# Tile shapes, key features and PSUM tensors of a sketched attention with an exact-GELU MLP

## Chip, cores and metric

The kernel runs on one core of a Trainium2 chip. The metric is the device time of one execution in microseconds (us); the median of three runs is given. One further execution is recorded by the hardware profiler, and all rows of engines come from that one. The engines are TensorE (PE, with its weight loads as PEld), VectorE (DVE), ScalarE (ACT), GpSimd (POOL) and SyncE (SP, which here only issues DMAs).

## The reference

```
phi(x): a = x S1^T, b = x S2^T (8 columns each); phi = all 64 products a_i b_j
kv  = sum over tokens of phi(k) v^T        (64 x 32, per batch and head)
z   = sum over tokens of phi(k)
x   = (phi(q) kv) / (phi(q) z + 1e-6)      (batch 4, heads 4, tokens 1088, head_dim 32)
h   = x' w_in                              (x' : 4352 tokens x 128, heads side by side)
out = gelu_exact(h) w_out                  (w_in 128 x 2048, w_out 2048 x 128)
```

Everything is float32; the two MLP weights and S1, S2 arrive as float64 words.

## The kernel before

**Chunks.** The 1024 main tokens of a batch are two chunks of 512, so chunks 0 to 7 are the main tokens and chunk 8 the 64 remaining tokens of all four batches (256 columns). For every chunk x^T (128 channels by tokens) is made by the attention, and then the MLP goes over 16 slices `fi` of 128 hidden features: `hidden` (L551) multiplies a slice of `w_in` with x^T into a PSUM bank and applies GELU on ACT (L558). Chunks 0 and 1 use `project` (L667) for the second product, summed in one PSUM bank over the 16 slices. Chunks 2 to 7 use seven-product blocks instead of eight (`two_products`, L624), with sums of the GELU blocks made on POOL (`token_sums`, L593 to L596) and of `w_out` (`channel_sums`), and `drain` and `combine` at the end. Chunk 8 has its own branch of `project` (L664).

**Steps.** The main loop goes over steps t, one per (chunk, fi). Chunks 0 and 1 take turns in groups of four slices (steps 0 to 31); then 16 steps per chunk. Products for the second matrix come `LAG` = 2 steps or more behind. All other work is hung on steps by hand with `at(t, ...)`: `query_turn` and `query_expand` (phi of the queries, L444, L453, L460, L474), `attend` (numerators and denominators L494, denominators copied L500, reciprocal L502, x^T L506), and for batches 1 to 3 the keys: `key_turn_blocks` (L333), `features`, that is `key_features` (products with S1 and S2 L348, the outer product L361 and L362), `add_tokens` (L383, L386), `finish_keys` (`kv_sum` L391, `kv_sum_rem` L420, `take_kv`), `turn_kv` (L429, L430). For chunk n from 3 on, t = 16 (n - 1) is the step at which chunk n - 1 begins; the odd n carry the keys of batch (n + 1) / 2, so chunk 3 those of batch 2 and chunk 5 those of batch 3.

At the end of the text each instruction is tied to the one before it on its engine, so that every engine keeps the order of the text. The framework adds the semaphores.

**Head.** Batch 0's keys and chunk 0 are written out ahead of the loop. `attend_by_token` (L520, L525, L526, L528) makes chunks 0 and 1 by token, and `turn_x` transposes them (L304) and copies the two halves of x^T with ACT (L533) and DVE (L534). `Rounding` turns float64 words of the weights into float32: fields (L252, L254, DVE), low words (L248, ACT), exponents (L260, ACT), mantissas (L268, DVE, or L265 on ACT and L266 on POOL), signs (L273, DVE), product (L278, DVE or POOL). `keep_busy` (L696) is idle work for PE.

**PSUM.** Of the eight banks `hps` holds two for `hidden`, `ops` two for sums, and `wps` two pairs (`work_banks()`; `halves` gives the two banks of a pair, `work_bank()` the first bank of a pair).

**Tile shapes.** A 128x128 matmul may be written as two over 64 columns of the weights each (`by_halves`), which the profile shows as 128*64. Each float32 matmul shows as two passes.

**Stores.** Results are turned on DVE and stored by SP (L687, L690); the last chunk is copied by DVE and ACT (L673) and stored by SP and ACT, two DMAs each (L675).

Of the kernel before, what the change touches and what calls it, by code (L numbers as in the profile page):

```python
# [8 lines left out]
FP = mybir.dt.float32  # L9
# [7 lines left out]
def kernel(  # L17
# [29 lines left out]
    JC = 4  # L47
# [31 lines left out]
    def out_bank():  # L79
        return ops.tile([128, CW], FP, name="o_ps")  # L80
# [154 lines left out]
    class Rounding:  # L235


        def __init__(self, dst):
            self.dst, self.wide = dst, dst.name in raw
            if self.wide:  # L240
                rows, n = dst.shape
                self.lo, self.hi = raw[dst.name][:, :, 0], raw[dst.name][:, :, 1]
                self.a, self.e, self.r = (mlp.tile([128, LC], U32, name=f"bits_{x}")[:rows, :n] for x in "aer")
                self.low, self.m = (mlp.tile([128, LC], FP, name=f"bits_{x}")[:rows, :n] for x in ("low", "m"))
# [55 lines left out]
    def transposed(ps, name, srcs, copy):  # L300

        n = len(srcs) * 128
        for i, s in enumerate(srcs):
            pe.transpose(ps[:, i * 128:(i + 1) * 128], in_=s, identity=ident)  # L304
        t = att.tile([128, CW], FP, name=name, bufs=3 if name == "xT" else 2)
        copy(out=t[:, :n], in_=ps[:, :n])
        return t
# [33 lines left out]

    def key_features(b, r, banks, by_pool=()):

        for i in range(2 * NCH):
            for c in range(2):
                for t in range(2):
                    at = i * 128 + c * 64
                    pe.matmul(banks[t][c * 64:(c + 1) * 64, i * 32:(i + 1) * 32],  # L348
                              lhsT=kT[r][t * 64:(t + 1) * 64, at:at + 64],
                              rhs=S12[t * 64:(t + 1) * 64, 2 * t:2 * t + 2].rearrange("p h r -> p (h r)"),  # L350
                              start=True, stop=True)

        k_p[b, r] = att.tile([128, 2, J, R, R], FP, name="k_p")
        a = att.tile([128, 2, J, 2 * R], FP, name="a_t")
        for t in (1, 0):
            ab = banks[t][:, :128].rearrange("p (n r) -> p n r", r=2 * R)
            if t in by_pool:
                act.copy(out=a[:, t], in_=ab)
                pool.tensor_mul(**spread(k_p[b, r][:, t], a[:, t, :, 0:R], a[:, t, :, R:2 * R]))
            else:  # L360
                act.copy(out=a[:, t, :, 0:R], in_=ab[:, :, 0:R])  # L361
                dve.tensor_mul(**spread(k_p[b, r][:, t], a[:, t, :, 0:R], ab[:, :, R:2 * R]))  # L362
# [65 lines left out]
    def turn_kv(b, ps, copy):  # L428
        pe.transpose(ps[:, :128], in_=kv_T[b], identity=ident)  # L429
        copy(out=kz[b].rearrange("p c n -> p (c n)"), in_=ps[:, :128])  # L430
# [55 lines left out]
    def attend(n, meanwhile=lambda: None):  # L486

        W = width[n]
        owners = [(0, W, n // NCH)] if n < NMAIN else [(i * REM, (i + 1) * REM, i % 2 * 2 + i // 2) for i in range(B)]
        banks = halves(work_banks())  # L490
        for (c0, c1, b) in owners:
            for c in range(NP):
                for r in range(2):
                    pe.matmul(banks[r][c * F:(c + 1) * F, c0:c1], lhsT=kz[b][r * F:(r + 1) * F, c, :],  # L494
                              rhs=qp[n][r * F:(r + 1) * F, c, c0:c1], start=True, stop=True)
        den = att.tile([128, CW], FP, name="den")
        for h in range(H):
            c, r = h // 2, h % 2
            at = c * F + (1 - r) * D
            act.activation(out=den[h * D:(h + 1) * D, :W], in_=banks[r][at:at + D, :W], func=ACT.Copy, bias=1e-6)  # L500
        meanwhile()
        dve.reciprocal(out=den[:, :W], in_=den[:, :W])  # L502
        xT[n] = att.tile([128, CW], FP, name="xT", bufs=3)
        for h in range(H):
            rows = slice(h * D, (h + 1) * D)
            dve.tensor_mul(out=xT[n][rows, :W], in0=banks[h % 2][rows, :W], in1=den[rows, :W])  # L506
# [23 lines left out]

    def turn_x(n, ps):
        def by_both(out, in_):
            by_act(out=out[:, :CW // 2], in_=in_[:, :CW // 2])  # L533
            by_dve(out=out[:, CW // 2:], in_=in_[:, CW // 2:])  # L534

        xT[n] = transposed(ps, "xT", [x_tok[n][:, j].rearrange("p h d -> p (h d)") for j in range(JC)], by_both)

# [47 lines left out]
    def token_sums(n, b):  # L585

        g = blocks[n, b].rearrange("p (e two) (half x) -> p e two half x", two=2, half=2)
        a11, a21, a12, a22 = (g[:, :, k, h] for k in range(2) for h in range(2))
        s = {}
        for j, (name, dtype) in enumerate((("bits_a", U32), ("bits_e", U32), ("bits_low", FP), ("bits_m", FP))):  # L590
            t = mlp.tile([128, LC], dtype, name=name)
            s[j + 1] = (t if dtype == FP else t.bitcast(FP)).rearrange("p (e x) -> p e x", e=2)
        pool.tensor_sub(out=s[3], in0=a11, in1=a21)  # L593
        pool.tensor_add(out=s[1], in0=a21, in1=a22)  # L594
        pool.tensor_sub(out=s[2], in0=s[1], in1=a11)  # L595
        pool.tensor_sub(out=s[4], in0=a12, in1=s[2])  # L596
        sums[n, b] = s
# [57 lines left out]

    def project(n, fi):
        first, final = fi == 0, fi == NF - 1
        if first:
            o_of[n] = out_bank() if n < NMAIN else work_bank()
        g = g_of.pop((n, fi))  # L660
        if n == NMAIN:

            for i in range(B // 2):
                pe.matmul(o_of[n][:, i * 128:(i + 1) * 128], lhsT=g[:, i * 128:(i + 1) * 128], rhs=w_tile(w_out_sb, fi),  # L664
                          start=(first and i == 0), stop=final, skip_group_check=True)
            return
        pe.matmul(o_of[n], lhsT=w_tile(w_out_sb, fi), rhs=g, start=first, stop=final)  # L667

    def store(n):
        oT = mlp.tile([128, JC, d_model], FP, name="oT")  # L670
        if n == NMAIN:
            for i, (copy, eng) in enumerate(((by_dve, sp), (by_act, act))):
                copy(out=oT[:, i, :], in_=o_of[n][:, i * 128:(i + 1) * 128])  # L673
                for b in (i, i + 2):
                    eng.dma_start(out=out[b * S + MAIN:(b + 1) * S, :], in_=oT[b // 2 * REM:(b // 2 + 1) * REM, i, :])  # L675
            return
# [69 lines left out]
    banks = [hidden_bank(), hidden_bank()]  # L746
    keep_busy(1, banks[0], 128)
    attend_by_token(0, banks)
    expand_products(1)
    bank = out_bank()  # L750
    keep_busy(1, bank)
    w_out = [Rounding(w) for w in w_out_sb[:2]]
    w_out[0].low_words()
# [4 lines left out]
    w_in[1].product(pool)  # L758
    w_out[0].fields()
    turn_x(0, hidden_bank())  # L760
    keep_busy(1, bank)
    w_out[0].exponents()
    expand_copy(1, 2)
    expand_multiply(1, 0)
    w_out[0].finish()
    w_out[1].low_words()

# [9 lines left out]
    def features(b, r):  # L777
        key_features(b, r, halves(work_banks()))

    held = {}  # L780
# [18 lines left out]

    at(0, expand_copy, 1, 3)  # L800
    at(0, expand_multiply, 1, 1)
    at(1, lambda: (w_out[1].fields(), w_out[1].exponents()))
    for i, (t0, t1) in enumerate(((4, 6), (8, 10), (12, 20))):
# [18 lines left out]
    for n in range(3, NCHUNK):  # L822
# [5 lines left out]
        at(t + 2 if n > 3 else t - 2, query_expand, n)  # L828
        at(t + 5, attend, n, lambda b=b, keys=keys: [key_turn_blocks(b, r) for r in range(2) if keys])
        if keys:  # L830
            at(t + 8, widen_v_rem, b)
            for r in range(2):
                at(t + 11, features, b, r)
            for r in range(2):
                at(t + 11, add_tokens, b, r, dve)
            at(t + 16, finish_keys, b)
            at(t + 17, lambda b=b: turn_kv(b, held["kv"], by_act))
# [5 lines left out]
    for t, (n, fi) in enumerate(steps):  # L843
        if n < FAST:
            products[t + LAG].append((project, n, fi))
            if fi == NF - 1:
# [16 lines left out]
    for t in range(len(steps) + LAG):  # L863
        if t == 3:

            attend_by_token(1, halves(work_banks()), lambda: (w_out[1].mantissas(), w_out[1].signs(),
                                                              w_out[1].product(pool)))
        if t == 4:
            turn_x(1, work_bank())
            for f, *a in products[t]:  # L870
                f(*a)
        for n in drains[t]:
            drain(n)
        if t < len(steps):
            n, fi = steps[t]
            hidden(n, fi, by_halves=n >= FAST and (n < NMAIN or fi < 5))
        if t < len(steps) and FAST <= steps[t][0] < NMAIN and steps[t][1] % NB == NB - 1:
# [49 lines left out]
```

## Time and profile before

| | |
|---|---|
| median of 3 runs | 278.13 us (277.85 to 278.22) |
| profiled execution | 278.03 us |
| its span, first to last instruction | 276.2 us |
| PE busy | 269.6 us, 2209 matmuls |
| DVE, ACT, POOL busy | 151.1, 142.9, 144.8 us |
| HBM read and written | 10.90 and 2.23 MB |
| granted TensorE clock, mean | 0.998 |

The costliest groups are L551 at 128*64 (384 passes of 512 columns, 98.7 us busy), L558 (96 GELUs of 597 ns), L624 and the POOL sums of about 1.28 us each. A matmul's busy time overlaps with its neighbours'; what it costs in a full stream is read from the chain of work that ended last, where each piece is the time from the end of the one before. "Idle before" in a row is how long the engine stood ahead of that instruction, and the arrow names what it waited for.

### The profile page before, as it was taken

To read this page: it belongs to the slowest core of one execution; us is meant where nothing else is said; L and a number is where in the kernel's file an instruction comes from. 1 tells how busy PE (TensorE), PEld (TensorE's weight loads), DVE (VectorE), ACT (ScalarE), POOL (GpSimd) and SP (SyncE) were. 2 spreads that over 40 slices of the span, in tenths; PEclk is the share of its full clock that TensorE was granted. 3 is DMA by queue.
4 is the path that set the end of the run, shared out by engine and by line. 5 is a ranking of instruction groups with operands and counts; after the bars stand their busy time and mean duration, and the time that the engine had idled before them with its cause. 6 is when DMAs were issued, how large, how long until landed. Compare 5 with 4: busy or idle time off the path is not lost.

```text
span 276.2 us, 5543 instructions
## 1 busy us (share of the span) xinstructions
PE 269.6 (98%) x2209; PEld 134.9 (49%) x2209; DVE 151.1 (55%) x248; ACT 142.9 (52%) x282; POOL 144.8 (52%) x158
## 2 busy tenths in 40 slices
PE   8989999999999999999999999999999999999993
PEld 6744444543432455445444555444444454455793
DVE  6987688424953565079308965479037902750230
ACT  4683764356454634484348433674358344733441
POOL 3331000952003896457875877368766886777300
PEclk9999999999999999999999999999999999999999
DMA  6659263636201200000200001000200020011020
GB/s 210 188 155 325 47 167 62 160 76 161 42 0 29 34 16 2 2 0 1 40 0 1 2 2 34 7 0 2 38 0 2 0 40 0 1 24 18 4 38 19
DMA packets 37914, 13.49 MB, mean 49 GB/s; under 512 B 28288, under 2 KB 37248, under 8 KB 37888
## 3 DMA queue, kind: packets, MB, share of 16 engines
q1 hardware_dynamic: 37648, 13.05, 18.8%
q8 instruction: 17, 0.28, 0.5%
q10 hardware_dynamic: 240, 0.08, 0.1%
q14 instruction: 9, 0.07, 0.1%
HBM read 10.90 MB, written 2.23 MB: 48 GB/s over the span
## 4 chain that ended last, share of the span: by engine, by line
PE 96%; DVE 2%; ACT 0%; issue 0%
PE h_ps L551 43%; PE o_ps L624 27%; PE o_ps L667 10%; PE w_ps L453 3%; PE w_ps L664 3%; PE w_ps L494 2%; PE w_ps L391 1%; PE w_ps L696 1%; PE w_ps L348 1%; PE o_ps L400 1%; PE h_ps L304 1%; PE h_ps L520 0%; PE w_ps L420 0%; PE w_ps L520 0%; PE o_ps L304 0%
## 5 line engine op out<-in xcount | busy, mean ns | idle before, releaser
L551 PE MATMUL h_ps<-xT,w_in 128*64 128x512 f32 (+3 forms) x490 | 141.0, 577 | 1.1 <-DVE xT L534 1.0
L558 ACT ACTIVATE block<-h_ps 128x512 f32<-128x512 f32 (+1 forms) x112 | 63.4, 566 | 84.6 <-PE h_ps L551 83.7
L551 PEld LDWEIGHTS h_ps<-xT,w_in 128*64 128x64 f32 (+1 forms) x490 | 43.2, 146 | 38.0 <-issue 14.4
L593 POOL TENSOR_TENSOR bits_low<-block 128x512 f32<-128x512 f32 x24 | 30.8, 1284 | 52.8 <-ACT block L558 52.6
L624 PE MATMUL o_ps<-block,w_out 128*64 128x256 f32 x192 | 49.5, 380 | 0.0
L474 DVE TENSOR_TENSOR q_pT<-A_sb,w_ps 64x512 f32<-64x512 f32 x32 | 22.1, 691 | 43.0 <-ACT A_sb L460 42.3
L624 PEld LDWEIGHTS o_ps<-block,w_out 128*64 128x64 f32 x192 | 25.7, 137 | 32.4 <-issue 24.5
L594 POOL TENSOR_TENSOR bits_a<-block 128x512 f32<-128x512 f32 x24 | 30.6, 1274 | 12.9 <-ACT block L558 12.8
L667 PE MATMUL o_ps<-g,w_out 128*128 128x512 f32 x64 | 33.5, 604 | 0.0
L596 POOL TENSOR_TENSOR bits_m<-block,bits_e 128x512 f32<-128x512 f32 x24 | 30.6, 1276 | 1.9
L595 POOL TENSOR_TENSOR bits_e<-bits_a,block 128x512 f32<-128x512 f32 x24 | 30.6, 1274 | 1.9
L558 ACT ACTIVATE g<-h_ps 128x512 f32<-128x512 f32 x32 | 19.1, 596 | 21.2 <-PE h_ps L551 21.1
L502 DVE RECIPROCAL den<-den 128x512 f32<-128x512 f32 (+1 forms) x7 | 21.8, 3115 | 10.7 <-ACT den L500 10.7
L624 PE MATMUL o_ps<-bits_a,small 128*64 128x256 f32 x96 | 24.9, 382 | 0.0
L624 PE MATMUL o_ps<-bits_low,small 128*64 128x256 f32 x96 | 24.7, 380 | 0.0
L624 PE MATMUL o_ps<-block,small 128*64 128x256 f32 x96 | 24.7, 380 | 0.0
L624 PE MATMUL o_ps<-bits_m,w_out 128*64 128x256 f32 x96 | 24.6, 379 | 0.0
L624 PEld LDWEIGHTS o_ps<-block,small 128*64 128x64 f32 x96 | 13.0, 137 | 15.8 <-issue 11.7
L460 ACT COPY A_sb<-w_ps 64x512 f32<-64x512 f32 (+1 forms) x36 | 17.7, 557 | 3.1 <-PE w_ps L453 2.9
L506 DVE TENSOR_TENSOR xT<-w_ps,den 32x512 f32<-32x512 f32 (+1 forms) x28 | 18.2, 649 | 1.0
L667 PEld LDWEIGHTS o_ps<-g,w_out 128*128 128x128 f32 x64 | 11.3, 190 | 14.5 <-issue 13.6
L500 ACT ACTIVATE den<-w_ps 32x512 f32<-32x512 f32 (+1 forms) x28 | 15.6, 557 | 2.0 <-PE w_ps L494 1.7
(158 smaller groups left out, 295.9 us busy)
## 6 DMA issues: line engine op xcount, KB each, us to landing
block<-in_moe_w_in_dram SPq DMA_DIRECT2D x3, 512.0 KB, 7.9
block<-in_moe_w_out_dram SPq DMA_DIRECT2D x3, 512.0 KB, 10.6
k<-in_k_dram SPq DMA_DIRECT2D x48, 32.0 KB, 1.8
v<-in_v_dram SPq DMA_DIRECT2D x3, 512.0 KB, 4.3
q<-in_q_dram SPq DMA_DIRECT2D x24, 64.0 KB, 3.8
out_dram<-oT SPq DMA_DIRECT2D x24, 64.0 KB, 2.2
k<-in_k_dram SPq DMA_DIRECT2D x2, 256.0 KB, 3.1
q<-in_q_dram SPq DMA_DIRECT2D x2, 256.0 KB, 4.2
```

The costliest lines, as they stand in the source:

```text
L460: act.copy(out=A[g // 2][F:, g % 2, :width[n]], in_=B_of[n][g // 2][:F, g % 2, :width[n]])
L474: dve.tensor_mul(out=cols[r * F:(r + 1) * F], in0=a[:, :, r::2], in1=b[:, :, r::2])
L502: dve.reciprocal(out=den[:, :W], in_=den[:, :W])
L506: dve.tensor_mul(out=xT[n][rows, :W], in0=banks[h % 2][rows, :W], in1=den[rows, :W])
L551: pe.matmul(ps[rows, :W], lhsT=w[:, rows], rhs=xT[n][:, :W], start=True, stop=True)
L558: act.activation(out=g_of[n, fi][:, :W], in_=ps[:, :W], func=ACT.Gelu)
L593: pool.tensor_sub(out=s[3], in0=a11, in1=a21)
L594: pool.tensor_add(out=s[1], in0=a21, in1=a22)
L595: pool.tensor_sub(out=s[2], in0=s[1], in1=a11)
L596: pool.tensor_sub(out=s[4], in0=a12, in1=s[2])
L624: pe.matmul(acc[n][bank][half * 64:(half + 1) * 64, col:col + HW], lhsT=fixed, rhs=moving, start=b == 0 and e == 0 and name in "4715", sto ...
L667: pe.matmul(o_of[n], lhsT=w_tile(w_out_sb, fi), rhs=g, start=first, stop=final)
```

## The change

- `Rounding` and `token_sums` get three buffers for `bits_a` and `bits_e`; transposed tiles have the width that they need.
- `key_features` is split into `key_products` (PE) and `key_outer` (ACT and DVE), with a column offset. For batches 2 and 3 the products of both r go into one pair of banks and stand in `attend`, right after its numerators (`features_of_all` as its `meanwhile`, now ahead of the denominators); `outer_of_all` follows in the same step, t + 5, where the features were at t + 11. `key_turn_blocks` moves from inside `attend` to t - 2.
- `turn_kv` of batches 2 and 3 is two 128x64 products with the identity instead of a transpose.
- `turn_x` transposes into two PSUM tensors, one for each copying engine.
- From step 8 on `hidden` and `project` of chunks 0 and 1 are in 128x64 halves, and those of chunk 8 to its end.
- Chunk 8's results lie in two PSUM tensors; each is copied and stored with one DMA.
- The head: fields of `w_out[0]` ahead of `attend_by_token(0)`, all of chunk 1's expansion ahead of the loop, the first four `hidden` of chunk 0 ahead of `attend_by_token(1)`, the rounding of `w_out[0]` and `w_out[1]` spread around them, and the first two `project` after it.

```diff
+            self.a, self.e, self.r = (... bufs=2 if x == "r" else 3 ...)
-    def key_features(b, r, banks, by_pool=()):
+    def key_features(b, r, banks, by_pool=(), col=0):
+        key_products(r, banks, col)
+        key_outer(b, r, banks, by_pool, col)
+    def key_outer(b, r, banks, by_pool=(), col=0):
         k_p[b, r] = att.tile([128, 2, J, R, R], FP, name="k_p")
         a = att.tile([128, 2, J, 2 * R], FP, name="a_t")
         for t in (1, 0):
-            ab = banks[t][:, :128].rearrange("p (n r) -> p n r", r=2 * R)
+            ab = banks[t][:, col:col + 128].rearrange("p (n r) -> p n r", r=2 * R)
...
     def turn_kv(b, ps, copy):
+        if b < 2:
+            pe.transpose(ps[:, :128], in_=kv_T[b], identity=ident)
+        else:
+            for rows in (slice(0, 64), slice(64, 128)):
+                pe.matmul(ps[rows, :128], lhsT=kv_T[b][:, rows], rhs=ident, start=True, stop=True)
...
     def attend(n, meanwhile=lambda: None):
...
                     pe.matmul(banks[r][c * F:(c + 1) * F, c0:c1], ...)
+        meanwhile()
         den = att.tile([128, CW], FP, name="den")
         for h in range(H):
...
-        meanwhile()
         dve.reciprocal(out=den[:, :W], in_=den[:, :W])
...
+    def turn_x(n, banks):
+        xT[n] = att.tile([128, CW], FP, name="xT", bufs=3)
+        for i, ps in enumerate(banks):
+            for j in range(2):
+                pe.transpose(ps[:, j * 128:(j + 1) * 128], in_=x_tok[n][:, 2 * i + j]..., identity=ident)
+        for i, (ps, copy) in enumerate(zip(banks, (by_act, by_dve))):
+            copy(out=xT[n][:, i * 256:(i + 1) * 256], in_=ps[:, :256])
...
-    def project(n, fi):
+    def project(n, fi, by_halves=False):
-            o_of[n] = out_bank() if n < NMAIN else work_bank()
+            o_of[n] = out_bank() if n < NMAIN else [work_bank() for i in range(B // 2)]
...
+        for rows in (slice(0, 64), slice(64, 128)) if by_halves else (slice(0, 128),):
+            pe.matmul(o_of[n][rows], lhsT=w[:, rows], rhs=g, start=first, stop=final)
...
-                for b in (i, i + 2):
-                    eng.dma_start(out=out[b * S + MAIN:(b + 1) * S, :], ...)
+                eng.dma_start(out=out.rearrange("(two i s) d -> i two s d", two=2, i=2)[i, :, MAIN:S, :],
+                              in_=oT[:, i, :])
...
+    def features_of_all(b):
+        banks = halves(work_banks())
+        for r in range(2):
+            key_products(r, banks, r * 128)
+        held["keys"] = banks
+    def outer_of_all(b):
+        for r in range(2):
+            key_outer(b, r, held["keys"], (), r * 128)
+        for r in range(2):
+            add_tokens(b, r, dve)
...
-        at(t + 5, attend, n, lambda b=b, keys=keys: [key_turn_blocks(b, r) for r in range(2) if keys])
+        if keys:
+            for r in range(2):
+                at(t - 2, key_turn_blocks, b, r)
+        at(t + 5, attend, n, lambda b=b, keys=keys: keys and features_of_all(b))
         if keys:
+            at(t + 5, outer_of_all, b)
             at(t + 8, widen_v_rem, b)
-            for r in range(2):
-                at(t + 11, features, b, r)
-            for r in range(2):
-                at(t + 11, add_tokens, b, r, dve)
...
-            products[t + LAG].append((project, n, fi))
+            products[t + LAG].append((project, n, fi, t + LAG >= 8))
...
+        if t < 4:
+            hidden(0, t)
+            if t == 0:
+                w_out[0].exponents()
+                w_out[0].finish()
+                w_out[1].fields()
+            if t == 3:
+                attend_by_token(1, halves(work_banks()), lambda: (w_out[1].exponents(), w_out[1].low_words(),
+                                                                  w_out[1].mantissas(by_pool=True)))
+                w_out[1].signs()
+                w_out[1].product()
+                for u in range(4):
+                    for f, *a in products[u]:
+                        f(*a)
+            continue
         if t == 4:
-            turn_x(1, work_bank())
+            turn_x(1, [work_bank(), work_bank()])
...
-            hidden(n, fi, by_halves=n >= FAST and (n < NMAIN or fi < 5))
+            hidden(n, fi, by_halves=t >= 8)
```

More of the change, by code (lines that the diff above doesn't have):

```diff
@@ L242, in __init__ @@
                 self.lo, self.hi = raw[dst.name][:, :, 0], raw[dst.name][:, :, 1]
-                self.a, self.e, self.r = (mlp.tile([128, LC], U32, name=f"bits_{x}")[:rows, :n] for x in "aer")
+                self.a, self.e, self.r = (mlp.tile([128, LC], U32, name=f"bits_{x}", bufs=2 if x == "r" else 3)[:rows, :n]
+                                          for x in "aer")
                 self.low, self.m = (mlp.tile([128, LC], FP, name=f"bits_{x}")[:rows, :n] for x in ("low", "m"))
@@ L304, in transposed @@
             pe.transpose(ps[:, i * 128:(i + 1) * 128], in_=s, identity=ident)
-        t = att.tile([128, CW], FP, name=name, bufs=3 if name == "xT" else 2)
-        copy(out=t[:, :n], in_=ps[:, :n])
+        t = att.tile([128, n], FP, name=name, bufs=1 if name == "kT_rem" else 2)
+        copy(out=t, in_=ps[:, :n])
         return t
@@ L340, in spread, with key_products @@
                     in1=b[:, :, None, :].broadcast_to([128, n, R, R]))
-    def key_features(b, r, banks, by_pool=()):
+    def key_features(b, r, banks, by_pool=(), col=0):
+        key_products(r, banks, col)
+        key_outer(b, r, banks, by_pool, col)
+    def key_products(r, banks, col=0):
         for i in range(2 * NCH):
@@ L347, in key_features @@
                     at = i * 128 + c * 64
-                    pe.matmul(banks[t][c * 64:(c + 1) * 64, i * 32:(i + 1) * 32],
+                    pe.matmul(banks[t][c * 64:(c + 1) * 64, col + i * 32:col + (i + 1) * 32],
                               lhsT=kT[r][t * 64:(t + 1) * 64, at:at + 64],
@@ L428, in turn_kv @@
     def turn_kv(b, ps, copy):
-        pe.transpose(ps[:, :128], in_=kv_T[b], identity=ident)
+        if b < 2:
[3 more added lines that the diff above has]
+                pe.matmul(ps[rows, :128], lhsT=kv_T[b][:, rows], rhs=ident, start=True, stop=True)
         copy(out=kz[b].rearrange("p c n -> p (c n)"), in_=ps[:, :128])
@@ L529, in attend_by_token @@
                            in1=den[:, r, :, None].broadcast_to([128, JC * NP, D]))
[L531 to L536, printed above, removed]
+    def turn_x(n, banks):
+        xT[n] = att.tile([128, CW], FP, name="xT", bufs=3)
+        for i, ps in enumerate(banks):
+            for j in range(2):
+                pe.transpose(ps[:, j * 128:(j + 1) * 128], in_=x_tok[n][:, 2 * i + j].rearrange("p h d -> p (h d)"),
+                             identity=ident)
+        for i, (ps, copy) in enumerate(zip(banks, (by_act, by_dve))):
+            copy(out=xT[n][:, i * 256:(i + 1) * 256], in_=ps[:, :256])
     g_of, o_of = {}, {}
@@ L590, in token_sums @@
         for j, (name, dtype) in enumerate((("bits_a", U32), ("bits_e", U32), ("bits_low", FP), ("bits_m", FP))):
-            t = mlp.tile([128, LC], dtype, name=name)
+            t = mlp.tile([128, LC], dtype, name=name, bufs=3 if dtype == U32 else 2)
             s[j + 1] = (t if dtype == FP else t.bitcast(FP)).rearrange("p (e x) -> p e x", e=2)
@@ L663, in project @@
             for i in range(B // 2):
-                pe.matmul(o_of[n][:, i * 128:(i + 1) * 128], lhsT=g[:, i * 128:(i + 1) * 128], rhs=w_tile(w_out_sb, fi),
-                          start=(first and i == 0), stop=final, skip_group_check=True)
+                for h in range(2):
+                    at = i * 128 + h * 64
+                    pe.matmul(o_of[n][i][h * 64:(h + 1) * 64, :128], lhsT=g[:, at:at + 64], rhs=w_tile(w_out_sb, fi),
+                              start=first, stop=final)
             return
-        pe.matmul(o_of[n], lhsT=w_tile(w_out_sb, fi), rhs=g, start=first, stop=final)
+        w = w_tile(w_out_sb, fi)
+        for rows in (slice(0, 64), slice(64, 128)) if by_halves else (slice(0, 128),):
+            pe.matmul(o_of[n][rows], lhsT=w[:, rows], rhs=g, start=first, stop=final)
     def store(n):
@@ L672, in store @@
             for i, (copy, eng) in enumerate(((by_dve, sp), (by_act, act))):
-                copy(out=oT[:, i, :], in_=o_of[n][:, i * 128:(i + 1) * 128])
-                for b in (i, i + 2):
-                    eng.dma_start(out=out[b * S + MAIN:(b + 1) * S, :], in_=oT[b // 2 * REM:(b // 2 + 1) * REM, i, :])
+                copy(out=oT[:, i, :], in_=o_of[n][i][:, :128])
+                eng.dma_start(out=out.rearrange("(two i s) d -> i two s d", two=2, i=2)[i, :, MAIN:S, :],
+                              in_=oT[:, i, :])
             return
@@ L747 @@
     keep_busy(1, banks[0], 128)
+    w_out = [Rounding(w) for w in w_out_sb[:2]]
+    w_out[0].fields()
     attend_by_token(0, banks)
@@ L751 @@
     keep_busy(1, bank)
-    w_out = [Rounding(w) for w in w_out_sb[:2]]
     w_out[0].low_words()
@@ L758 @@
     w_in[1].product(pool)
-    w_out[0].fields()
-    turn_x(0, hidden_bank())
+    turn_x(0, [hidden_bank(), hidden_bank()])
     keep_busy(1, bank)
[L762 to L766, printed above, removed]
+    for i in range(2):
+        for g in range(2):
+            if i:
+                expand_copy(1, 2 + g)
+        expand_multiply(1, i)
     steps = [(n, fi) for f in range(0, NF, 4) for n in range(2) for fi in range(f, f + 4)]
@@ L798, in round_at @@
         at(t + 1, lambda: (r[0].exponents(), r[0].finish()))
-    at(0, expand_copy, 1, 3)
-    at(0, expand_multiply, 1, 1)
-    at(1, lambda: (w_out[1].fields(), w_out[1].exponents()))
     for i, (t0, t1) in enumerate(((4, 6), (8, 10), (12, 20))):
@@ L863 @@
     for t in range(len(steps) + LAG):
-        if t == 3:
-            attend_by_token(1, halves(work_banks()), lambda: (w_out[1].mantissas(), w_out[1].signs(),
-                                                              w_out[1].product(pool)))
+        if t < 4:
[13 more added lines that the diff above has]
+            continue
         if t == 4:
-            turn_x(1, work_bank())
+            turn_x(1, [work_bank(), work_bank()])
             for f, *a in products[t]:
```

## The prediction

> **What bounds the kernel now.** I read the page first: the busy times, then the shares of the chain that ended last.
>
> ```profile
> PE 269.6 (98%) x2209; PEld 134.9 (49%) x2209; DVE 151.1 (55%) x248; ACT 142.9 (52%) x282; POOL 144.8 (52%) x158
> PE 96%; DVE 2%; ACT 0%; issue 0%
> ```
>
> TensorE is the bound from end to end; every other engine is half idle. So time can only be won where PE does less or waits less, and it is lost wherever another engine makes PE wait. Next the chain of waits in order of time (start, us, what), around the attention of chunk 3 (`attend`, L494) and the key features of batch 2 (L348):
>
> ```profile
> 89.20 1.02 PE w_ps L494 x8
> 90.22 1.01 PE h_ps L551 x4
> 91.23 1.29 PE o_ps L624 x12
> 92.52 0.86 PE h_ps L551 x4
> 93.38 0.86 PE o_ps L624 x8
> ...
> 100.27 1.06 PE w_ps L348 x64
> 101.33 0.58 PE o_ps L624 x4
> ```
>
> One hidden product L551 costs 0.86 us, whether as two 128x128 passes (x2) or four 128x64 ones (x4). After another tile shape the same work costs more: L551 1.01, L624 0.58 for 0.43, and 1.06 for an L667 at 128x128. I read a change of shape as 0.15 us into 128x64 and 0.20 us into 128x128.
>
> The timeline of the same stretch on ACT and DVE (start, us, instruction, idle before it and releaser):
>
> ```profile
> 90.28 2.38 ACT L500 ACTIVATE den<-w_ps 32x512 f32<-32x512 f32 x4 [0.44 <-PE w_ps L494]
> 92.69 1.33 ACT L558 ACTIVATE block<-h_ps 128x512 f32<-128x512 f32 x2
> 92.70 3.35 DVE L502 RECIPROCAL den<-den 128x512 f32<-128x512 f32 x1 [4.94 <-ACT den L500]
> 96.16 2.79 DVE L506 TENSOR_TENSOR xT<-w_ps,den 32x512 f32<-32x512 f32 x4
> ...
> 100.93 0.21 ACT L361 COPY a_t<-w_ps 128x64 f32<-128x64 f32 x1
> 101.25 0.69 DVE L362 TENSOR_TENSOR k_p<-a_t,w_ps 128x512 f32<-128x512 f32 x1 [2.30 <-ACT a_t L361]
> 101.97 0.33 ACT L361 COPY a_t<-w_ps 128x64 f32<-128x64 f32 x2 [0.82 <-DVE k_p L362]
> 102.21 1.29 DVE L362 TENSOR_TENSOR k_p<-a_t,w_ps 128x512 f32<-128x512 f32 x2 [0.28 <-ACT a_t L361]
> 103.53 0.21 ACT L361 COPY a_t<-w_ps 128x64 f32<-128x64 f32 x1 [1.24 <-DVE k_p L362]
> ```
>
> See the brackets of the second and third L361 lines: ACT's copy of one half (t = 0) waits for DVE's product of the other half (t = 1), though the halves are different banks. Both lie in one PSUM tensor `w_ps`. Batch 0 has its halves in two tensors, and there the two copies run back to back before any product:
>
> ```profile
> 7.19 0.33 ACT L361 COPY a_t<-o_ps 128x64 f32<-128x64 f32 x2 [0.86 <-PE o_ps L348]
> ```
>
> The list of waits agrees: ACT L361 waited for DVE L362 six times, twice per batch 1 to 3. Readers of one PSUM tensor on two engines take turns in text order. The head and the end show the same turn-taking (L534 behind L533, ACT's L673 behind DVE's), as well as PE's one real wait:
>
> ```profile
> 18.29 2.97 PE L551 MATMUL h_ps<-xT,w_in 128*128 128x512 f32 x6 [1.03 <-DVE xT L534]
> 26.15 0.42 DVE L534 COPY xT<-w_ps 128x256 f32<-128x256 f32 x1 [1.15 <-ACT xT L533]
> ...
> 272.42 0.27 ACT L673 COPY oT<-w_ps 128x128 f32<-128x128 f32 x1 [1.28 <-DVE oT L673]
> 272.71 1.18 ACTq L675 DMA_DIRECT2D out_dram<-oT  x2
> ```
>
> **What the Trainium skill says.** "TensorEngine Tiling (Array Packing)", Key Properties: changing the tiling mode drains TensorE. The trace agrees (0.15 to 0.20 us). "PSUM — Partial Sum Buffer", Terms: two engines must not touch one bank and quadrant at once, reads included; different banks are not named. The trace is stricter: the wait is there across banks of one tensor, so it is the program's semaphores that serialize. "TensorE: Matmul & The Clock Gate": the table at the top calls ScalarE's queue strictly first-in first-out (the trace agrees: no GELU passes a waiting copy), and What's actually happening says that an idle window of about 3.4 us halves PE's clock until it has been busy about as long. No idle time that long is in this trace, but the cold start is: six idle products took 2.93 us from 1.20 and eight transposes 1.58, against 0.215 and 0.11 each later, so about 4.4 us at half rate.
>
> **The change part by part**, against the profiled execution (span 276.24, 278.03 with what lies around it; the median of the runs is 278.13, 0.1 above).
>
> *Head.* DVE's two fields of `w_out[0]` (0.28 each) move from ahead of xT into the 0.54 us that DVE idles before den_tok at 14.73: cost 0 to 0.05, and their load was issued at 7.33 with 4.5 us to landing. The second x^T half then follows bits_e, which ends at 16.85, and ends at about 17.3; ACT's half ends at 17.37 as now. So the first L551 starts at 17.45 instead of 18.29. Then in order of PE's ends: two hidden products to 19.33; the third 20.29; the fourth waits for the GELU of the second, which now has two A_sb copies (0.53 each) and bits_r ahead of it on ACT, 21.4; L520 1.07, 22.5; two L667 with 0.20 for the shape, 24.4; four transposes 0.43; L667 0.86; two hidden products 1.72: 27.4. The chain of before has the same work done at 28.61. `w_out[1]` must be ready at 24.8: its add moves to POOL (0.72) and its product from POOL to DVE (0.43); I get 24.7, so it just hides. **-1.2** (-0.6 to -1.5). The loads keep their place; no DMA moves.
>
> *128x64 in chunks 0 and 1 from step 8.* L551/L667 alternating at the seam of chunk 1 to 2 (81.42 to 89.20) carry 0.15+0.20+0.15+0.20+0.20: -0.9. Returns after L348, L453 (twice), L494 become 0.15: -0.2. After L420 there is none: -0.2. Against it one entry (0.15) and the full-array transposes L304, L429 and the product L369, which now switch in and out: 0.3, 0.3, 0.25. **-0.3** (0 to -0.6).
>
> *Keys next to the attention* (batches 2 and 3): L348 follows L494, both 64x64, so an entry (about 0.18) and a return (0.15) go: **-0.65** for two. *`turn_kv` in halves*, two: 0.26+0.15 becomes two pairs of 128 columns, 0.22: **-0.4**. *Last chunk*: no return to 128x128 at 259.96: **-0.2**. Its L664 as halves isn't shown; between 0.43 per step (pairs as in L624) and 0.87 (no pairing); L420's eight halves in 0.38, switch included, say pairing. *End*: the copies run side by side, and each queue issues one store instead of two (0.59 each; 64 KB ones of L690 0.65): ACT's last issue starts at about 272.4 instead of 273.3: **-0.9** (-0.4 to -1.0). The third buffers of bits_a and bits_e cost nothing. Moving `key_turn_blocks` to t-2 puts 4 x 0.41 us of DVE ahead of a stretch where DVE is half idle; the last K load is issued at 63.6, the first use comes at 78.
>
> Together **-3.65**.
>
> *What the key features wait for.* `outer_of_all` is put right behind `attend`. On ACT its four copies stand behind the four den and ahead of the next GELU; on DVE its products stand behind reciprocal and xT. Copy 2 waits for product 1, as L361 does now, and all four copies now read one tensor. With E the end of L494 (90.22): den ends E+2.44, copy 1 runs; reciprocal starts E+2.48, xT ends E+8.73; product 1 ends E+9.45; three more turns of 0.03+0.24+0.69 bar the last product, copy 4 ends E+11.6; the GELU that stood at 92.69 ends E+12.24, and PE can have its bank at about E+12.34. Two hidden banks: PE goes on with L348 0.88, L551 1.01, L624 1.29, L551 0.86, L624 0.86, in all E+4.90, and then stands. **7.44 us**, plus 0.16 until the first product is through. Nothing else fills it: PE takes its queue in order. The GELU, done at 93.3 in before, has 1.8 us of slack there; it comes 9.2 later. Chunk 5 has the same rows (L494 ends 149.91, den 2.38). PE has then idled over 3.4 us; at half rate for 4.4 us it loses 2.2 more (0 to 3.4). That is 9.8 each, **+19.6** for two.
>
> Sum: 278.03 - 3.65 + 19.6 = 294.0.
>
> **Rivals.** *The copies don't wait* (faster): the halves' reads at L361 are released by bank, so ACT is held for 4 x 0.21 only. Then the gains stand: 274.4. It decides if copy 2 starts before product 1 ends; break-even is 1.8 us of standing per batch. For it: the banks differ. Against it: six waits of six in before, with the same tensor shape. *The clock stays up*: 7.6 each, 289.6; for it that no warm gap is in the trace, against it the cold start. *The change doesn't do what it says*: 128x64 tiles for all chunks change next to nothing, since both shapes cost 0.86; without any gain 297.6.
>
> **How the numbers follow.** Standing with a slow restart 0.68, without 0.20, no wait 0.09, something between (one batch only, 283 to 287) 0.03. The range runs from 288 (no clock loss, gains of 4.2) to 297.5 (3.4 of clock loss each, gains of 2.6). About 0.2% (0.6 us) is what a measurement tells here: slower 0.90, faster 0.09, within 0.01.
>
> **What would show it.** In the profile after: ACT L361 of batches 2 and 3 waiting 6 to 7 us for DVE L362, L551 waiting for ACT some 7 us in two places, more time for the products just behind; x^T halves side by side; one store per queue. Wrong if PE shows no gap behind L348.

## The result and the profile after

The changed kernel takes 297.07 us (296.25 to 297.53) against 278.18 us (medians of four runs each): ratio 1.0674, 95% interval 1.0643 to 1.0705. The forecast was 294.0 us (288.0 to 297.5). The profiled execution took 297.40 us with a span of 295.6, so 19.4 us came on top of the 278.03 before; the page and all rows below are of that execution. Lines have moved: L551 is now L566, L558 is L573, L624 is L639, L361 and L362 are L368 and L369, L494 is L506, L667 is L686, L673 is L692, L675 is L693.

The page after, its busy times, the granted clock in 40 slices and the chain by engine:

```profile
PE 273.3 (92%) x2401; PEld 131.4 (44%) x2401; DVE 156.6 (53%) x248; ACT 142.8 (48%) x283; POOL 146.8 (50%) x158
...
PEclk9999999999999579999999869999999999999999
...
PE 89%; DVE 6%; ACT 3%; issue 1%; DVEq 0%
```

In the kernel before, the chain was TensorE nearly alone (96%). Now DVE and ACT hold 9% of it, and the clock drops in two places. The chain of waits around the first of them (start, us, what):

```profile
87.94 1.06 PE w_ps L506 x8
...
91.44 3.37 DVE den L514
...
97.72 0.70 DVE k_p L369
98.42 0.02 issue
98.44 0.22 ACT a_t L368
...
100.66 0.51 ACT block L573
101.17 0.04 issue
101.21 1.98 PE h_ps L566 x4
103.19 1.71 PE o_ps L639 x8
104.89 1.71 PE h_ps L566 x4
106.60 1.14 PE o_ps L639 x8
107.74 0.86 PE h_ps L566 x4
```

The chain leaves PE after the numerators, runs over den, reciprocal, x^T and the key products, and returns to PE through one GELU (L573, listed as `block`). The timeline of the same stretch on ACT and PE (idle before, and what ended it, in brackets):

```profile
91.44 0.21 ACT L368 COPY a_t<-w_ps 128x64 f32<-128x64 f32 x1
98.44 0.21 ACT L368 COPY a_t<-w_ps 128x64 f32<-128x64 f32 x1 [6.79 <-DVE k_p L369]
99.41 0.21 ACT L368 COPY a_t<-w_ps 128x64 f32<-128x64 f32 x1 [0.75 <-DVE k_p L369]
100.44 0.21 ACT L368 COPY a_t<-w_ps 128x64 f32<-128x64 f32 x1 [0.82 <-DVE k_p L369]
100.55 1.09 ACT L573 ACTIVATE block<-h_ps 128x512 f32<-128x512 f32 x2
...
101.21 1.98 PE L566 MATMUL h_ps<-xT,w_in 128*64 128x512 f32 x4 [7.32 <-ACT block L573]
```

The second copy stands 6.79 us for DVE's first product, the two GELUs stand behind the copies, and PE stands 7.32 us for the first of them. At chunk 5 the copy stands 6.80 us and PE 7.25. The list of waits adds both:

```profile
PE h_ps L566 <- ACT block L573: 14.6, 2, 7.3
```

A table of windows gives for each stretch its length, the busy times of PE, PEld, DVE, ACT and POOL, and then the mean granted clock (1.00 is full), the busy share of the DMA engines and GB/s. Here are the first gap and what follows it, then the same around the second:

```profile
94.00:101.20 7.20, 0.00 (x0) 0.00 (x0) 6.12 (x9) 1.18 (x5) 0.00 (x0) 0.69 0.22 35
101.20:104.90 3.70, 3.69 (x14) 1.70 (x16) 3.67 (x4) 1.04 (x2) 3.59 (x3) 0.50 0.03 5
104.90:107.70 2.80, 2.80 (x14) 1.13 (x14) 2.77 (x3) 0.60 (x1) 2.66 (x4) 0.62 0.00 0
107.70:111.20 3.50, 3.50 (x26) 1.56 (x24) 0.46 (x1) 1.19 (x2) 2.01 (x5) 1.00 0.00 0
...
163.60:170.70 7.10, 0.00 (x0) 0.00 (x0) 6.09 (x9) 1.16 (x5) 0.00 (x0) 0.84 0.00 0
170.70:174.40 3.70, 3.67 (x14) 1.68 (x16) 3.67 (x4) 1.06 (x2) 3.57 (x3) 0.50 0.00 0
174.40:175.80 1.40, 1.40 (x8) 0.41 (x6) 1.36 (x2) 0.00 (x0) 1.32 (x2) 0.68 0.00 0
```

The clock is at 0.50 behind both gaps and back at 1.00 a few microseconds later.

The head has the two x^T halves side by side and four hidden products in a row, from the timeline:

```profile
16.79 0.42 DVE L551 COPY xT<-h_ps 128x256 f32<-128x256 f32 x1 [0.18 <-PE h_ps L548]
16.80 0.37 ACT L551 COPY xT<-h_ps 128x256 f32<-128x256 f32 x1
17.36 3.83 PE L566 MATMUL h_ps<-xT,w_in 128*128 128x512 f32 x8 [0.18 <-DVE xT L551]
```

The end holds the surprise. The two last copies also run side by side and each queue issues one store, but the span goes on for 5.7 us behind ACT's copy, where it was 3.6 before. Timeline of the end, then the rates and packets of its last 7 us (the row of rates has 40 equal slices; the rows of the queues give packets, MB and the share of 16 DMA engines' time that the packets took):

```profile
289.60 0.27 ACT L692 COPY oT<-w_ps 128x128 f32<-128x128 f32 x1 [0.93 <-PE w_ps L681]
289.89 0.64 ACTq L693 DMA_DIRECT2D out_dram<-oT  x1
```

```profile
GB/s 0 0 0 0 0 0 0 0 0 0 0 20 29 41 47 41 47 41 32 35 47 41 44 44 41 47 41 44 44 23 0 0 0 0 0 0 0 0 0 0
DMA packets 260, 0.13 MB, mean 19 GB/s; under 512 B 4, under 2 KB 260, under 8 KB 260
q1 hardware_dynamic: 130, 0.07, 3.4%
q10 hardware_dynamic: 130, 0.07, 3.1%
```

The same rows of the kernel before, over its last 5 us:

```profile
GB/s 0 0 0 0 0 0 0 0 0 0 0 0 20 160 82 94 148 25 148 107 62 164 41 0 0 0 0 0 0 0 0 0 0 0 0 0 0 0 0 0
DMA packets 320, 0.13 MB, mean 26 GB/s; under 512 B 64, under 2 KB 320, under 8 KB 320
q1 hardware_dynamic: 160, 0.07, 5.0%
q10 hardware_dynamic: 160, 0.07, 4.9%
```

For the same bytes the stores before are busy in 11 slices of 0.125 us, 1.4 us in all, with peaks of 164 GB/s. After, they are busy in 19 slices of 0.175 us, 3.3 us in all, and never pass 47 GB/s. The packets themselves take about as long in sum (an estimate from the shares: 9.9% of 16 engines over 5 us are 7.9 us, 6.5% over 7 us are 7.3 us). So about 6 engines were at work at a time before, and about 2 after.

### The profile page after: what moved, and what is told of

Its sections match the earlier page's. It is cut to its first block, busy times and chain, and to the rows that moved or that the text cites. A ratio compares the mean times of both kernels' runs of the same rounds, so it can differ in the third digit from the quotient of the medians.

```text
span 295.6 us, 5929 instructions
## 1 busy us (share of the span) xinstructions
PE 273.3 (92%) x2401; PEld 131.4 (44%) x2401; DVE 156.6 (53%) x248; ACT 142.8 (48%) x283; POOL 146.8 (50%) x158
## 4 chain that ended last, share of the span: by engine, by line
PE 89%; DVE 6%; ACT 3%; issue 1%; DVEq 0%
PE h_ps L566 40%; PE o_ps L639 24%; PE o_ps L686 10%; PE w_ps L464 3%; PE w_ps L681 2%; PE w_ps L506 2%; DVE den L514 2%; DVE xT L518 2%; ACT den L513 2%; DVE k_p L369 1%; PE w_ps L398 1%; PE w_ps L715 1%; PE o_ps L407 1%; PE h_ps L532 0%; ACT a_t L368 0%
## 5 line engine op out<-in xcount | busy, mean ns | idle before, releaser
L566 PE MATMUL h_ps<-xT,w_in 128*64 128x512 f32 (+2 forms) x560 | 144.0, 582 | 14.7 <-ACT block L573 14.6
L573 ACT ACTIVATE block<-h_ps 128x512 f32<-128x512 f32 (+1 forms) x112 | 63.2, 566 | 89.9 <-PE h_ps L566 89.3
L566 PEld LDWEIGHTS h_ps<-xT,w_in 128*64 128x64 f32 (+1 forms) x560 | 41.1, 141 | 53.0 <-ACT block L573 19.3
L639 PE MATMUL o_ps<-block,w_out 128*64 128x256 f32 x192 | 51.3, 391 | 0.0
L639 PEld LDWEIGHTS o_ps<-block,w_out 128*64 128x64 f32 x192 | 26.5, 141 | 34.3 <-issue 26.9
L609 POOL TENSOR_TENSOR bits_a<-block 128x512 f32<-128x512 f32 x24 | 31.4, 1309 | 13.9 <-ACT block L573 13.8
L686 PE MATMUL o_ps<-g,w_out 128*64 128x512 f32 (+1 forms) x116 | 33.2, 600 | 0.1
L611 POOL TENSOR_TENSOR bits_m<-block,bits_e 128x512 f32<-128x512 f32 x24 | 31.3, 1304 | 1.9
L573 ACT ACTIVATE g<-h_ps 128x512 f32<-128x512 f32 x32 | 19.1, 597 | 22.0 <-PE h_ps L566 22.0
L639 PE MATMUL o_ps<-bits_m,w_out 128*64 128x256 f32 x96 | 26.4, 401 | 0.0
L639 PE MATMUL o_ps<-bits_low,small 128*64 128x256 f32 x96 | 25.0, 383 | 0.0
L639 PE MATMUL o_ps<-block,small 128*64 128x256 f32 x96 | 25.0, 383 | 0.0
L639 PE MATMUL o_ps<-bits_a,small 128*64 128x256 f32 x96 | 24.9, 382 | 0.0
L639 PEld LDWEIGHTS o_ps<-block,small 128*64 128x64 f32 x96 | 13.5, 141 | 16.8 <-issue 12.7
L686 PEld LDWEIGHTS o_ps<-g,w_out 128*64 128x64 f32 (+1 forms) x116 | 8.9, 142 | 15.2 <-issue 14.8
```

The lines of the kernel that those rows point to most:

```text
L566: pe.matmul(ps[rows, :W], lhsT=w[:, rows], rhs=xT[n][:, :W], start=True, stop=True)
L573: act.activation(out=g_of[n, fi][:, :W], in_=ps[:, :W], func=ACT.Gelu)
L639: pe.matmul(acc[n][bank][half * 64:(half + 1) * 64, col:col + HW], lhsT=fixed, rhs=moving, start=b == 0 and e == 0 and name in "4715", sto ...
L686: pe.matmul(o_of[n][rows], lhsT=w[:, rows], rhs=g, start=first, stop=final)
```

## The experiments

The ratios are to runs of the kernel before that were timed alongside (median 278.20 us for the first four experiments, 278.21 for the others). The theory to be tested: ACT's copies take turns with DVE's products because both read one PSUM tensor, and DVE's products stand behind reciprocal and x^T.

**Copies first.** `outer_of_all` of the changed kernel is written out with the four copies ahead of the four products; nothing else moves.

```diff
     def outer_of_all(b):
+        todo = []
         for r in range(2):
...
             for t in (1, 0):
                 act.copy(out=a[:, t, :, 0:R], in_=ab[:, :, 0:R])
-                dve.tensor_mul(**spread(k_p[b, r][:, t], a[:, t, :, 0:R], ab[:, :, R:2 * R]))
+                todo.append(spread(k_p[b, r][:, t], a[:, t, :, 0:R], ab[:, :, R:2 * R]))
+        for product in todo:
+            dve.tensor_mul(**product)
```

> The changed kernel, with one thing moved in the text: for batches 2 and 3 the four ACT copies of the keys come first and the four DVE products after them. Same step, same PSUM tensor, same instructions. If PE stands because a copy waits its turn behind DVE's product of the same PSUM tensor, and DVE is still at reciprocal and x^T: no wait of ACT for DVE is left there, PE has no gap, and all of 7.3 + 0.3 + 2.8 and 7.3 + 0.3 + 2.2 us goes: 297.1 - 20.1 = 277.0 us. If instead ACT simply has too much in one step (four den, four copies, a GELU): the work is all still there, and it stays above 290 us.

Measured 277.61 us, ratio to before 0.9977 (0.9968 to 0.9986). The timeline of ACT:

```profile
91.56 0.56 ACT L812 COPY a_t<-w_ps 128x64 f32<-128x64 f32 x4
91.98 0.64 ACT L573 ACTIVATE block<-h_ps 128x512 f32<-128x512 f32 x1
```

Four copies now take 0.56 us together and the GELU follows at once; the list of PE's waits has no GELU left in it. All instructions are still in the same step, on the same engines, with the same tensor: 19.5 us (297.07 - 277.61) of the loss was the order of the text alone. The load of the step is out.

**Keys back at t + 11**, in the changed kernel:

```diff
-        at(t + 5, attend, n, lambda b=b, keys=keys: keys and features_of_all(b))
+        at(t + 5, attend, n, lambda b=b, keys=keys: [key_turn_blocks(b, r) for r in range(2) if keys])
         if keys:
-            at(t + 5, outer_of_all, b)
+            for r in range(2):
+                at(t + 11, features, b, r)
+            for r in range(2):
+                at(t + 11, add_tokens, b, r, dve)
```

> The changed kernel with the key features put back to step t + 11 in two pairs of banks and the key transposes back inside the attention, everything else as changed. Both the turn-taking and the too-much-in-one-step theory: no gap of PE, and the two merged tile shapes (0.31 us each) lost: 277.6 us. If the stop comes from another part (halves, third buffers, head), it stays near 297.

Measured 278.31 us, ratio 1.0002 (0.9993 to 1.0011): PE waits for no GELU. Next to copies first, the place of the key products right behind the numerators, with what moved along with it, is worth 278.31 - 277.61 = 0.70 us; the intervals do not touch. Without the key part the whole remaining change takes as long as the kernel before, so something in it gives back what the head was expected to win.

**The key part alone**, in the kernel before (the split of `key_features`, `meanwhile` ahead of den, `features_of_all`, `outer_of_all`, transposes at t - 2, as in the diff of the change).

> The kernel before with only the key part of the change (products of both r in one pair of banks right after the numerators, outer products in the same step, transposes at t - 2). Turn-taking: this part alone makes both gaps, 278.1 + 20.1 - 0.6 = 297.6 us. If the gaps need the rest of the change: about 277.5.

Measured 297.04 us in one run. Its list of waits has the two gaps, the same to the tenth:

```profile
PE h_ps L557 <- ACT block L564: 14.6, 2, 7.3
```

So the key part is enough by itself; neither the halves nor the third buffers are needed.

**Products ahead of the reciprocal.** The turns between copy and product stay; only what DVE does first is changed.

```diff
             act.activation(out=den[h * D:(h + 1) * D, :W], ...)
+        then()
         dve.reciprocal(out=den[:, :W], in_=den[:, :W])
...
-        at(t + 5, attend, n, lambda b=b, keys=keys: keys and features_of_all(b))
+        at(t + 5, attend, n, lambda b=b, keys=keys: keys and features_of_all(b),
+           lambda b=b, keys=keys: keys and outer_of_all(b))
```

> The changed kernel, with the outer products of the keys (copy, product, copy, product as changed) put between the denominators and the reciprocal, so that DVE does them first and copies still take turns with products. Turn-taking: GELU ends some 6.2 us behind the last numerator instead of 12.2, PE stands about 1.4 us at each of two places, too short for the half clock: 277.0 + 2 x 1.65 = 280.3 us. If any stop at all halves the clock for some microseconds: about 285. If the load of the step is what counts: no better than 297.

Measured 280.39 us, ratio 1.0079 (1.0069 to 1.0088). The second copy still waits for a product, but for 0.82 us instead of 6.79. That row, the list of PE's waits, and the window around the first stop with the clock (1.00):

```profile
92.89 0.21 ACT L368 COPY a_t<-w_ps 128x64 f32<-128x64 f32 x1 [0.82 <-DVE k_p L369]
```

```profile
PE h_ps L567 <- ACT block L574: 2.6, 2, 1.3
```

```profile
94.00:101.00 7.00, 5.65 (x42) 2.77 (x40) 6.49 (x6) 3.06 (x7) 5.17 (x5) 1.00 0.22 35
```

The length of the stop follows what DVE has ahead of the first product: 1.3 us each with nothing, 7.3 with reciprocal and x^T. A stop of 1.3 us left the clock at 1.00; one of 7.3 us halved it. No stop between these two was tried.

**Two stores per queue**, on top of copies first:

```diff
-                eng.dma_start(out=out.rearrange("(two i s) d -> i two s d", two=2, i=2)[i, :, MAIN:S, :],
-                              in_=oT[:, i, :])
+                for b in (i, i + 2):
+                    eng.dma_start(out=out[b * S + MAIN:(b + 1) * S, :], in_=oT[b // 2 * REM:(b // 2 + 1) * REM, i, :])
```

> Copies first (the run before), and the last chunk stored again with two DMAs of 64 rows per queue instead of one whose rows come in two groups. In the changed kernel the span ends 6.0 us after PE's last product, 4.2 in the kernel before, and the two last DMAs moved at some 45 GB/s instead of some 150. If the DMA with two groups as its outer dimension is what is slow (few of the 16 engines work on it): the end is 4.2 less the 0.3 of the copies side by side, so 277.6 - 2.1 = 275.5 us. If the bytes or the copies set the end: no gain, 277.6, or a loss of 0.6 for the second issue.

Measured 275.46 us, ratio 0.9899 (0.9885 to 0.9913): 1% below the kernel before, and so faster than both kernels. Timeline and packets of its end:

```profile
269.55 1.25 ACTq L694 DMA_DIRECT2D out_dram<-oT  x2
```

```profile
DMA packets 320, 0.13 MB, mean 19 GB/s; under 512 B 64, under 2 KB 320, under 8 KB 320
```

The second issue costs its 0.6 us, and the end is still shorter: in the profiles it is 3.9 us from PE's last product to the end of the span, against 6.0 with copies first alone. The medians differ by the same 2.15 us. A DMA of 64 rows brings 16 small packets (64 in 4 DMAs), one with two groups of rows 2 (4 in 2 DMAs). So I read that the rows of a DMA are dealt out over engines by its outermost dimension, 64 in one case and 2 in the other. That fewer engines were at work is read from the shares above; that the outermost dimension decides it is not shown, as a DMA with another number of groups was not tried.

**Last results in one PSUM tensor**, in its two banks, on top of two stores:

```diff
-            o_of[n] = out_bank() if n < NMAIN else [work_bank() for i in range(B // 2)]
+            o_of[n] = out_bank() if n < NMAIN else halves(work_banks())
```

> As e5_two_stores, but the last chunk's results in the two banks of one PSUM tensor instead of two tensors. If readers of one tensor take turns across its banks here too: ACT's copy waits for DVE's, 0.3 us more than e5, 275.8. If only readers of one bank do: the same as e5.

Measured 275.82 us, ratio 0.9914 (0.9900 to 0.9928), which overlaps the run above, so the time does not tell them apart. The timelines do. First ACT's copy with two tensors (the run above), then with one:

```profile
269.25 0.27 ACT L692 COPY oT<-w_ps 128x128 f32<-128x128 f32 x1 [0.93 <-PE w_ps L681]
...
271.03 0.27 ACT L696 COPY oT<-w_ps 128x128 f32<-128x128 f32 x1 [1.25 <-DVE oT L696]
```

With two tensors ACT's copy waits only for PE; with one it waits for DVE's copy, although the two read different banks in both runs. So it is the tensor to which the banks belong in the program that decides, not the bank.

**Whole tiles in chunks 0 and 1**, on top of two stores:

```diff
-            products[t + LAG].append((project, n, fi, t + LAG >= 8))
+            products[t + LAG].append((project, n, fi))
-            hidden(n, fi, by_halves=t >= 8)
+            hidden(n, fi, by_halves=n >= FAST)
```

> As e5_two_stores, with all products of chunks 0 and 1 at 128x128 as in the kernel before (chunk 8 stays in halves). The prediction gave the halves a gain of 0.3 us, the chain of the changed kernel reads as 0.13: 275.6 to 275.8, no more than the noise above e5. If the shape itself mattered, with 0.86 us per product either way being misread, it would be several us.

Measured 275.02 us, ratio 0.9901 (0.9884 to 0.9917): no difference from halves that the intervals can tell.

**The head of before**, on top of two stores (the text of the head and steps 0 to 4 as in the kernel before, x^T of a chunk in one PSUM tensor).

> As e5_two_stores, with the head of the kernel before (order of rounding, expansion and first products, x^T of one chunk in one PSUM tensor). The prediction gave the head 1.2 us, the chains read as 1.0 to 1.1: 276.5 us.

Measured 276.65 us, ratio 0.9939 (0.9925 to 0.9954), so the head is worth 1.2 us by the medians. The chains show the first two hidden products of chunk 1. With the head of before they end at 26.36 + 1.98 = 28.34:

```profile
26.36 1.98 PE h_ps L563 x4
```

and with that of the change at 25.53 + 1.72 = 27.25:

```profile
25.53 1.72 PE h_ps L566 x4
```

That is 1.1 us. The clock at the start (last section) has little part in it: the eight first transposes took 1.30 and 1.25 us.

## Why the prediction was right, and which terms were off

The mechanism is the one that it named, shown from two sides: taking the turns away removes it, and the key part alone makes it.

That the total came out inside the range is in part luck. At 297.07 it lies 0.4 us below the upper end of 297.5, which had been drawn for a larger loss of clock and smaller gains, not for the slow end that took it there. The lower end is a slip besides: no clock loss with gains of 4.2 and the two stands of 7.6 us gives 278.03 - 4.2 + 15.2 = 289.0, not 288.

- **The wait.** Predicted: copy 2 waits for product 1, the GELU ends at E+12.24, PE stands 7.44 us. Measured: the GELU ends at E+12.17 (101.17 against 89.00), and PE stands 7.32 and 7.25 us. The sum of rows that already stood in the profile before was good to 0.2 us.
- **The clock.** Predicted 2.2 us each, from the slow products at the start of the kernel. Behind the first gap 1.98+1.71+1.71+1.14 stand where four times 0.86 would, 3.10 more, of which 0.26 is the first product's way through: 2.84 lost. Behind the second 1.98+1.71+1.36 stand for three, 2.21 lost without the 0.26. The Trainium skill, "TensorE: Matmul & The Clock Gate", What's actually happening, names an idle window of about 3.4 us; the traces agree on both sides (7.3 us: 0.50; 1.3 us: 1.00). The rival in which the clock stays up fell. That the second gap lost just the 2.2 us is chance, for the two losses differ for a reason that the sum did not have: the clock changes on a grid of 3.41 us, and the gaps lie differently on it (last section).
- **The rival without waits between banks** fell: in both steps every copy behind the first waited for a product, and in the last chunk ACT's copy waited again when both banks were put in one tensor.
- **Head.** Predicted -1.2; 1.19 between the medians of the two runs, 1.1 in their chains.
- **Key products next to the numerators.** Predicted -0.65; 0.70 between the medians of the two runs.
- **Chunks 0 and 1.** Predicted -0.3; the stretch from the second hidden product of chunk 1 to the end of the sixteen passes ahead of L506 takes 60.46 us (27.48 to 87.94) against 60.59 (28.61 to 89.20). Nearly nothing, as both shapes cost 0.86; in this part the third rival was right.
- **`turn_kv` and the last chunk.** Predicted -0.4 and -0.2. In the chain the transpose in halves reads 0.22 where 0.26+0.15 stood, so 0.19 each were won; a step of L681 takes 0.44 in halves as it did whole, so the pairing held.
- **The end is the term that failed**, though the total stayed in the range. It was put at -0.9, counting issues and copies. From PE's last product to the end of the span it was 4.2 us before and is 6.0 after: +1.8, off by 2.7. I priced the store by its issue time (0.65 predicted, 0.64 measured) and took the transfer as unchanged since the bytes were. What the transfer took is what was mis-sized: with the copies side by side and two stores per queue again, the end is 3.9 us, so the merged store costs 2.1 us net, the saved issue included. That term is most of the 3.4 us between the sum (294.0) and the profiled execution (297.4); half a microsecond more is in the two gaps.

The end is also what gave back the head's gain: with the keys at t + 11, where the merged store was still in, the kernel stood at 278.31, no better than before.

## What to carry to other kernels

Before moving an instruction forward on one engine, ask what its partner has queued ahead on the other: two engines that read one PSUM tensor in turns tie their queues together, and a 0.2 us copy can hold everything behind it for as long as the other engine's whole backlog. Put all reads of one engine first (tried here), or lay the parts in tensors of their own (seen here with the last chunk; for the key features of batches 2 and 3 it was not tried). Price a DMA by how it spreads over the engines as well as by its issue: fewer DMAs of the same bytes can end later, as the merged stores did here.

## What the runs showed of the hardware

- PE's clock changes on a grid in time. In the changed kernel short windows put its steps at 96.80 (down), 107.04 (up), 168.48 (down) and 175.30 us (up). The distances are 10.24, 61.44 and 6.83 us: 3, 18 and 2 times 3.41; a last step down, at 294.77, is 35 such spacings later. With the key part alone the steps are at 97.53, 107.77, 169.21 and 176.04, the same distances. PE had stopped at 93.89 and 163.48, so the clock fell 2.9 and 5.0 us into the two gaps, and the half rate lasted 5.8 and 4.6 us behind them. That is why two nearly equal gaps lost 2.84 and 2.21 us.
- The start moves with that grid too. Counted back in steps of 3.4133 us (from 96.80 in the changed kernel, in the others from the step down behind the last product), the grid has a step at 4.64 us in the changed kernel, 5.45 in the kernel before (from 275.10), 5.47 with copies first (271.70) and 6.29 with the products ahead of the reciprocal (275.94). The eight first transposes, which begin at 4.12, took 1.19, 1.58, 1.59 and 1.71 us, in the same order. (The views show the clock as 1.00 there, so the slow start is read from the times of the products alone.) With two stores they took 1.25, and the first hidden product started at 17.13 us, against 17.48 with copies first and the same text of the head. A difference of 0.35 us in a head can be this alone.
- The last chunk's 0.13 MB moved in 3.3 us, at no more than 47 GB/s, as one store of 128 rows in two groups per queue. As two stores of 64 rows per queue they moved in 1.4 us in the kernel before, with peaks of 164 GB/s, and reached 152 in the run with two stores.
- Reads of two engines from different banks of one PSUM tensor were done in turn (ACT idle for 6.79 and 1.25 us until DVE was done); from two tensors they ran side by side (289.38 and 289.60 us in the last chunk).
